# Eight heads' scores and v's weight summary as 64x32 pieces, in an attention with two expert layers

## The chip, the cores and the metric

The kernel runs on one core of a Trainium2 chip. The time is device microseconds of one execution. A profile comes from one more execution, with every engine's instructions recorded. The engines are TensorE (PE, with its weight loads as PEld), VectorE (DVE), ScalarE (ACT), GpSimd (POOL) and SyncE (SP), which issues the transfers.

## What is computed

```python
# q, k, v: (8, 8, 576, 64)   phi: (8, 8, 576, 32)
a = phi - np.max(phi, axis=2, keepdims=True)
a = np.exp(a)
a = a / (np.sum(a, axis=2, keepdims=True) + 1e-09)
k_m = np.einsum('bhsm,bhsd->bhmd', a, k)
v_m = np.einsum('bhsm,bhsd->bhmd', a, v)
scores = scale * np.matmul(q, k_m.transpose(0, 1, 3, 2))
scores = scores - np.max(scores, axis=-1, keepdims=True)
attn = np.exp(scores)
attn = attn / (np.sum(attn, axis=-1, keepdims=True) + 1e-09)
x = np.matmul(attn, v_m)      # heads side by side: (4608, 512)
h = x @ w_in                  # (4608, 2048)
x = (h * (1.0 / (1.0 + np.exp(-1.702 * h)))) @ w_out
h = x @ w2_in
out = (h * (1.0 / (1.0 + np.exp(-h)))) @ w2_out
```

There are 8 batches of 8 heads. A head's k and v are summed over the sequence into 32 rows of 64 each (the summaries), and q is scored against k's.

## The kernel before

**Two layers.** The first part of the program runs attention and the first expert layer together, in 256 slots; a batch has 32, a half sequence (288 tokens, `HS`) 16. In a slot, `first1` makes one block of 128 of the 2048 hidden features with six matmuls (L386: two groups of four heads, three products of high and low halves each), `gate` passes it through tanh (ScalarE, L360), one VectorE step (L361), a rounded copy (ScalarE, L364) and the rest (POOL, L366), and two slots later (`LAG`) `second1` multiplies it by the output weights with twelve matmuls (L398). The second expert layer follows from slot 256 on (from about 820 us), in another form, and has no part in the change.

**Attention's matmuls are folded into the first weight.** attn @ v_m @ w_in is computed as attn @ (v_m @ w_in). `wp_mm` (L276) makes that product w', 512 hidden features at a time (`c`, four of them) and four heads at a time (`g`, two); `wp_hi` (ScalarE, L281) and `wp_lo` (VectorE, L285) split it into a rounded half and the rest, the `slab`, which L386 reads as its stationary side. The moving side is `attnT`, the softmax of the scores, transposed.

**How heads lie.** `kv_mm` (L185) makes the summaries of four heads at once, each in 32 columns of the array, so a bank holds four heads x 32 rows. `kv_norm` divides by the sums and writes each row twice, side by side, once in the first and once in the second 64 columns; a mask (0 or 1 by partition) keeps one of the two, so that after the transposition by `kv_t` and the copy by `kv_e` a pair of heads stands block by block in `kvT`. One matmul over 128 rows (two heads x 64) and 64 columns then serves a pair of heads: `scores` (L230) and `wp_mm` (L276) each make two of them for four heads, one into each half of the partitions of one PSUM bank. `q_t` (L220) transposes q by pairs of heads, `q_e` copies that into `qT`.

**Softmax.** `soft1` transposes the scores out of PSUM in 32x32 blocks (VectorE, L242), takes the maximum (L244) and subtracts it (L245); `soft_exp` is on ScalarE; `soft2` sums, divides and transposes back; `soft_hi` and `soft3` split the result into `attnT`.

**PSUM.** All of attention's matmuls share two banks in turn (`ps_a`, 2 buffers, taken by `psa()`). A bank is free again when its reader on ScalarE or VectorE is through.

**What sets the order.** Tables of slot numbers. In a slot, the steps planned for "e" are written first, then `first1`, the steps for "p" (attention's matmuls), those for "l", `second1` of two slots ago, and those for "d" (transfers, all on SP's queue in the order written). `W0`, `W1`, `WS` hold w's slots of batch 0, of batch 1 and of the later ones, `QS` those of q, `SC` those of scores, `soft1` and `soft2`, counted from the batch's own start `z`; `ATT0`, `Q0` are for batch 0, which begins 46 slots ahead of slot 0. Up to slot 33 a scheduler may reorder the steps; from slot 34 on (`MANUAL`) each engine runs them as written.

Of the kernel before, what the change touches and what calls it, by code (L numbers as in the profile page):

```python
# [8 lines left out]
F32 = mybir.dt.float32  # L9
# [5 lines left out]
ALU = mybir.AluOpType  # L15
# [6 lines left out]
def attn_moe_moe(ctx: ExitStack, tc: tile.TileContext, q, k, v, phi, w1i, w1o, w2i, w2o, out):  # L22
    nc = tc.nc
    B, H, S, D = q.shape
# [167 lines left out]
    def kv_norm(b, g):  # L192
        a = st.pop(("kvps", b, g))
        rs = att.tile([128, 2], F32, tag="rs", name="rs", bufs=2)
        nc.vector.tensor_scalar(out=rs[:, 0:1], in0=a[:, 2 * D:2 * D + 1], scalar1=1e-9, scalar2=None, op0=ALU.add)
        nc.vector.reciprocal(out=rs[:, 1:2], in_=rs[:, 0:1])
        kvb = att.tile([128, 2, 2, D], F32, tag="kvb", name="kvb")
        keep = mask.rearrange("p (s o) -> p s o", o=1).to_broadcast([128, 2, D])
        for i in range(2):
            x = a[:, i * D:(i + 1) * D].rearrange("p (o d) -> p o d", o=1).to_broadcast([128, 2, D])  # L200
            nc.vector.scalar_tensor_tensor(out=kvb[:, i], in0=x, scalar=rs[:, 1:2], in1=keep,
                                           op0=ALU.mult, op1=ALU.mult)
        st["kvb", b, g] = kvb

    def kv_t(b, g):
# [14 lines left out]
            nc.tensor.transpose(a[:, c * P:(c + 1) * P], src[:, c], ident[:P, :P])  # L220

    def q_e(b, hf, p):
        t = att.tile([128, P, C3], F32, tag="qT", name="qT", bufs=3)
        nc.scalar.copy(out=t, in_=st.pop(("qp", b, hf, p))[:, 0:HS].rearrange("p (c s) -> p s c", c=C3))
        st["qT", b, hf, p] = t

    def scores(b, hf, g):
        a = st["sp", b, hf, g] = psa()
        for i in range(2):
            nc.tensor.matmul(out=a[64 * i:64 * i + 64, 0:HS],  # L230
                             lhsT=st["kvT", b, g][:, 0, 64 * i:64 * i + 64],
                             rhs=st.pop(("qT", b, hf, 2 * g + i)).rearrange("p s c -> p (s c)"),
                             start=True, stop=True)

    NG = HS // 32

# [33 lines left out]
        t = attnT[b, hf]  # L270
        (nc.gpsimd if b else nc.vector).tensor_tensor(out=t[:, g, 1], in0=x, in1=rd(t[:, g, 0]), op=ALU.subtract)

    def wp_mm(b, c, g):
        a = st["wp", b, c, g] = psa()
        for i in range(2):
            nc.tensor.matmul(out=a[64 * i:64 * i + 64], lhsT=st["kvT", b, g][:, 1, 64 * i:64 * i + 64],  # L276
                             rhs=w1[:, 2 * g + i, c * 512:(c + 1) * 512], start=True, stop=True)

    def wp_hi(b, c, g):
        t = slab[b, c, g] = moe.tile([128, 2, 512], F32R, tag="slab", name="slab", bufs=8)  # L280
# [409 lines left out]

    A0 = -46
    INIT = 'PABwwCDwwqqqq'
    Q0 = (-25, -14, -10, -7, -2, 0, 3, 3)
    LQ0 = (-7, -7, -4, 0)
    ATT0 = ((-9, -8, -7), (-6, -5, -3), (1, 2, 6), (5, 6, 7))


    LOAD = (None, None, None, None, -15, -15, -14, -10, -10, -9, -10, -8, -7, -5, -5, -4, -1, -3, 0, 1, 1, 4, 6,
# [29 lines left out]
    def plan_attention(b, z):  # L728
        for g in range(2):
            at(z - 2 + g, "e", phi_max, b, g)  # L730
        at(z + 1, "p", phi_max_t, b)
        at(z + 2, "e", phi_max_r, b)
        at(z + 3, "p", phi_max_b, b)
        for g in range(2):
            at(z + 4 + g, "e", phi_sub, b, g)
            at(z + 5 + g, "e", phi_exp, b, g)
            at(z + 6 + g, "e", phi_sum, b, g)
        for g, (k0, k1, n, t, e) in enumerate(KV):
            at(z + k0, "p", kv_mm, b, g, 0)
            at(z + k1, "p", kv_mm, b, g, 3)  # L740
            at(z + n, "e", kv_norm, b, g)
            todo.setdefault((z + t, "p"), []).insert(0, (kv_t, (b, g)))
            at(z + e, "e", kv_e, b, g)
        at(z + 10, "d", load_kv, b, 1, 0)
        at(z + 11, "d", load_kv, b, 1, 3)
        if b + 1 < B:
            at(z + 14, "d", load_kv, b + 1, 0, 0)
            at(z + 15, "d", load_kv, b + 1, 0, 3)
            at(z + 15, "d", load_phi, b + 1)
        for n in range(8):  # L750
            at(z + QS[n], "p", q_t, b, n // 4, n % 4)
            at(z + QS[n] + 1, "e", q_e, b, n // 4, n % 4)
            at(z + (QS[n - 2] if n > 1 else 2 + n), "d", load_q, b, n // 4, n % 4)
        for n, (p, s1, s2) in enumerate(SC):
            at(z + p, "p", scores, b, n // 2, n % 2)
            at(z + s1, "e", soft1, b, n // 2, n % 2)
            at(z + s1, "l", soft_exp, b, n // 2, n % 2)
            at(z + s2, "e", soft2, b, n // 2, n % 2)
            at(z + s2, "l", soft_hi, b, n // 2, n % 2)
            at(z + s2 + 1, "e", soft3, b, n // 2, n % 2)  # L760

    def plan_first(z):

        for g in range(2):
            at(z, "e", phi_max, 0, g)
            at(z + 3, "e", phi_sub, 0, g)
            at(z + 3, "l", phi_exp, 0, g)
            at(z + 4, "e", phi_sum, 0, g)
        at(z + 1, "p", phi_max_t, 0)
        at(z + 2, "e", phi_max_r, 0)  # L770
        at(z + 2, "p", phi_max_b, 0)
        for g in range(2):
            at(z + 4 + g, "p", kv_mm, 0, g, 0)
            at(z + 4 + g, "p", kv_mm, 0, g, 3)
            at(z + 5 + g, "e", kv_norm, 0, g)
            at(z + 6 + g, "p", kv_t, 0, g)
            at(z + 7 + g, "e", kv_e, 0, g)
        at(0, "d", load_phi, 1)
        at(5, "d", load_kv, 1, 0, 0)
        at(5, "d", load_kv, 1, 0, 3)  # L780
        for n in range(8):
            at(Q0[n], "p", q_t, 0, n // 4, n % 4)
            at(Q0[n] + 1, "e", q_e, 0, n // 4, n % 4)
            if n > 3:
                at(LQ0[n - 4], "d", load_q, 0, n // 4, n % 4)
        for n, (p, s1, s2) in enumerate(ATT0):
            at(p, "p", scores, 0, n // 2, n % 2)
            at(s1, "e", soft1, 0, n // 2, n % 2)
            at(s1, "l", soft_exp, 0, n // 2, n % 2)
            at(s2, "e", soft2, 0, n // 2, n % 2)  # L790
            at(s2, "l", soft_hi, 0, n // 2, n % 2)
            at(s2 + 1, "e", soft3, 0, n // 2, n % 2)

    def plan_wprime(b, n, s):
        a = (b,) + divmod(n, 2)
        at(s, "p", wp_mm, *a)
# [16 lines left out]
    for x in INIT:  # L813
# [42 lines left out]
    z = 32 * (B - 1) + 5  # L856
# [159 lines left out]
```

## Time and profile before

| what | |
|---|---|
| median of three runs | 1579.01 us (1578.94 to 1579.07) |
| the profiled execution | 1581.45 us |
| its span, first to last instruction | 1579.7 us |
| PE busy | 1511.9 us |
| DVE busy | 1010.7 us |
| ACT busy | 765.2 us |
| POOL busy | 567.9 us |
| w' matmuls (L276), 256 records | 72.8 us |
| scores matmuls (L230), 128 records | 25.9 us |

A float32 matmul leaves two records on PE, one for each of its passes. Busy time counts a stretch once, however many instructions overlap in it, and the ends of matmuls are modelled, so what a step costs TensorE is better read from the distance between starts than from its busy time.

### The profile page before, as it was taken

The page shows a single profiled execution, that of the slowest core. Times are in us where ns is not written, and L with a number is a line of the kernel's source. Part 1 is how long each engine was busy: PE and PEld are TensorE (multiplying, and loading weights), DVE is VectorE, ACT ScalarE, POOL GpSimd, SP SyncE. Part 2 cuts the span into 40 slices and gives each one's busy share as a digit, 9 for nine tenths or more (in the row PEclk, how much of TensorE's full clock was granted, in tenths as well). Part 3 has the DMA queues.
Part 4 walks back from the last instruction along what each step waited for, and adds up shares of the span by engine and source line. Part 5 has one row for each costly group of instructions (what it writes and reads, how often), then busy time and mean ns, then how long its engine had stood idle before and what let it go on. Part 6 is the DMA issues. An engine that isn't in the chain of part 4 may idle for free.

```text
span 1579.7 us, 29100 instructions
## 1 busy us (share of the span) xinstructions
PE 1511.9 (96%) x11104; PEld 1406.2 (89%) x11104; DVE 1010.7 (64%) x1552; ACT 765.2 (48%) x1539; POOL 567.9 (36%) x469
## 2 busy tenths in 40 slices
PE   4799999999999999999999999999996999999998
PEld 2578898888989889898998999999986999999998
DVE  6996546365473554635467656556577788878875
ACT  4664344454454445444455554555554344444443
POOL 2764334344343444433322323123124343142140
PEclk9899999999999999999999999999998999999999
DMA  9652242523525244221124334334455325335230
GB/s 283 182 163 65 57 130 71 158 76 94 139 87 145 69 125 112 89 62 42 60 75 155 121 134 147 110 141 147 135 191 175 118 93 191 104 107 191 89 122 31
DMA packets 174156, 189.08 MB, mean 120 GB/s; under 512 B 50112, under 2 KB 161728, under 8 KB 174016
## 3 DMA queue, kind: packets, MB, share of 16 engines
q1 hardware_dynamic: 174016, 187.22, 38.5%
q8 instruction: 87, 1.43, 0.4%
q14 instruction: 53, 0.43, 0.1%
HBM read 122.16 MB, written 65.01 MB: 118 GB/s over the span
## 4 chain that ended last, share of the span: by engine, by line
PE 79%; DVE 7%; issue 4%; ACT 4%; DMA 3%; POOL 2%; SPq 1%; DVEq 0%; ACTq 0%; POOLq 0%
PE y L398 23%; PE p L646 21%; PE h L386 11%; PE xb L533 9%; PE y L533 6%; PE a L276 3%; PE a L185 2%; PE a L230 1%; DVE e L435 1%; ACT xq L523 1%; PE a L220 1%; DMA raw<-in_moe_w_out_dram 1%; ACT gq L542 1%; DMA wst<-w2s 1%; POOL r L435 1%
## 5 line engine op out<-in xcount | busy, mean ns | idle before, releaser
L398 PE MATMUL y<-gh,wo 128*128 128x288 f32 x2048 | 460.1, 301 | 0.4 <-ACT gh L364 0.3
L398 PEld LDWEIGHTS y<-gh,wo 128*128 128x128 f32 x2048 | 341.4, 188 | 52.2 <-issue 25.8
L646 PE MATMUL p<-wq,op 128*128 128x256 f32 x3024 | 367.3, 284 | 14.0 <-ACT op L631 9.6
L646 PEld LDWEIGHTS p<-wq,op 128*128 128x128 f32 x3024 | 365.0, 191 | 16.4 <-ACT op L631 10.5
L366 POOL TENSOR_TENSOR gl<-g,gh 128x288 fp32r<-128x288 f32 x256 | 225.6, 882 | 425.3 <-ACT gh L364 386.1
L398 PE MATMUL y<-gl,wo 128*128 128x288 f32 x1024 | 301.9, 295 | 2.5 <-POOL gl L366 2.5
L361 DVE SCALAR_TENSOR_TENSOR g<-g,h 128x288 f32<-128x288 f32 x256 | 114.7, 449 | 289.5 <-ACT g L360 288.8
L438 DVE TENSOR_TENSOR op<-r,op 128x768 fp32r<-128x768 f32 x168 | 225.7, 1365 | 74.9 <-ACT op L631 74.3
L386 PE MATMUL h<-attnT,slab 128*128 128x288 f32 x1536 | 250.7, 298 | 12.9 <-ACT attnT L266 4.9
L386 PEld LDWEIGHTS h<-attnT,slab 128*128 128x128 f32 x1536 | 219.1, 189 | 19.0 <-ACT attnT L266 6.8
L533 PE MATMUL xb<-xq,wq 128*128 128x384 f32 x1152 | 220.7, 340 | 11.9 <-ACT e L583 7.2
L631 ACT CAST op<-r 128x768 fp32r<-128x768 f32 x168 | 139.3, 837 | 169.4 <-PE p L646 122.4
L533 PEld LDWEIGHTS xb<-xq,wq 128*128 128x128 f32 x1152 | 201.4, 189 | 19.9 <-ACT e L583 12.2
L360 ACT ACTIVATE g<-h 128x288 f32<-128x288 f32 x256 | 104.1, 407 | 191.3 <-PE h L386 185.4
L398 PEld LDWEIGHTS y<-gl,wo 128*128 128x128 f32 x1024 | 192.8, 188 | 4.4 <-POOL gl L366 3.4
L364 ACT CAST gh<-g 128x288 fp32r<-128x288 f32 x256 | 110.7, 433 | 167.9 <-DVE g L361 167.9
L533 PE MATMUL y<-xq,wq 128*128 128x384 f32 x864 | 166.1, 336 | 0.0
L533 PEld LDWEIGHTS y<-xq,wq 128*128 128x128 f32 x864 | 151.5, 188 | 0.3 <-ACT e L594 0.3
L542 ACT ACTIVATE gq<-e 128x384 f32<-128x384 f32 x144 | 75.0, 526 | 135.8 <-DVE e L435 134.5
L435 POOL TENSOR_TENSOR r<-r 128x768 f32<-128x768 f32 x24 | 55.9, 2353 | 193.7 <-DMA r<-gs 193.6
L547 DVE SCALAR_TENSOR_TENSOR gq<-gq,e 128x384 f32<-128x384 f32 x144 | 97.1, 680 | 35.1 <-ACT gq L542 29.7
L438 POOL TENSOR_TENSOR xq<-xr,xq 128x768 fp32r<-128x768 f32 x20 | 38.5, 1926 | 134.0 <-ACT xq L523 134.0
(111 smaller groups left out, 1535.2 us busy)
## 6 DMA issues: line engine op xcount, KB each, us to landing
gs<-gq SPq DMA_DIRECT2D x192, 192.0 KB, 1.9
r<-gs SPq DMA_DIRECT2D x192, 192.0 KB, 4.2
raw<-in_moe_w_out_dram SPq DMA_DIRECT2D x24, 512.0 KB, 4.3
raw<-in_moe_w_in_dram SPq DMA_DIRECT2D x18, 512.0 KB, 4.5
xr<-xs SPq DMA_DIRECT2D x24, 384.0 KB, 5.3
out_dram<-o SPq DMA_DIRECT2D x24, 384.0 KB, 3.6
q<-in_q_dram SPq DMA_DIRECT2D x124, 72.0 KB, 2.5
kv<-in_k_dram SPq DMA_DIRECT2D x30, 288.0 KB, 4.7
```

The source lines that it names most:

```text
L360: nc.scalar.activation(out=t[:, :n], in_=h[:, :n], func=ACTF.Tanh, scale=c)
L361: nc.vector.scalar_tensor_tensor(out=t[:, :n], in0=t[:, :n], scalar=1.0, in1=h[:, :n], op0=ALU.add, op1=ALU.mult)
L364: nc.scalar.copy(out=gh[:, :n], in_=t[:, :n])
L366: nc.gpsimd.tensor_tensor(out=gl[:, :n], in0=t[:, :n], in1=rd(gh[:, :n]), op=ALU.subtract)
L386: nc.tensor.matmul(out=h[:, :HS], lhsT=slab[b, f // 4, g][:, wi, f0:f0 + 128], rhs=x[:, g, xi], start=(g == 0 and n == 0), stop=(g == 1 an ...
L398: nc.tensor.matmul(out=ybank[d][:, :HS], lhsT=w[:, wi, d * 128:(d + 1) * 128], rhs=gg[gi][:, :HS], start=(f == fa and n == 0), stop=(f == ...
L438: eng.tensor_tensor(out=out, in0=a, in1=b, op=ALU.subtract)
L533: nc.tensor.matmul(out=out, lhsT=w[:, s, wi, f0:f0 + 128], rhs=x[:, s, xi], start=(start and s == 0 and k == 0), stop=(s == 1 and k == 2), ...
L542: nc.scalar.activation(out=t, in_=h, func=ACTF.Tanh)
L547: nc.vector.scalar_tensor_tensor(out=t, in0=t, scalar=1.0, in1=h, op0=ALU.add, op1=ALU.mult)
L631: nc.scalar.copy(out=t[:, :, 0], in_=s)
L646: nc.tensor.matmul(out=out[:, d], lhsT=t[:, u, gi, d * 128:(d + 1) * 128], rhs=w[:, u, wi], start=(start and d != 1 and p == 0 and u == 0 ...
```

## The change

A matmul of attention now takes one head: 64 rows and 32 columns of the array. A new function, `pairs`, writes eight of them, for all eight heads, over four column strips (`j`) and two row halves (`s`); those of the first row half go to one PSUM bank and those of the second to the other. `scores` and `wp_mm` call it, so each is one step for eight heads where it was two steps for four. A bank now holds the four even heads or the four odd ones, in scores and in w' alike. The two copies that `kv_norm` writes are both kept, in one VectorE instruction and without the mask, and `kvb` shares the buffer of `at`. `qT` gets a fourth buffer. The steps have new slots.

```diff
-        kvb = att.tile([128, 2, 2, D], F32, tag="kvb", name="kvb")
-        keep = mask.rearrange("p (s o) -> p s o", o=1).to_broadcast([128, 2, D])
-        for i in range(2):
-            x = a[:, i * D:(i + 1) * D].rearrange("p (o d) -> p o d", o=1).to_broadcast([128, 2, D])
-            nc.vector.scalar_tensor_tensor(out=kvb[:, i], in0=x, scalar=rs[:, 1:2], in1=keep,
-                                           op0=ALU.mult, op1=ALU.mult)
+        kvb = att.tile([128, HS], F32, tag="at", name="kvb")[:, 0:4 * D].rearrange("p (i s d) -> p i s d", i=2, s=2)
+
+        x = a[:, 0:2 * D].rearrange("p (i o d) -> p i o d", i=2, o=1).to_broadcast([128, 2, 2, D])
+        nc.vector.tensor_scalar(out=kvb, in0=x, scalar1=rs[:, 1:2], scalar2=None, op0=ALU.mult)
...
-    def scores(b, hf, g):
-        a = st["sp", b, hf, g] = psa()
-        for i in range(2):
-            nc.tensor.matmul(out=a[64 * i:64 * i + 64, 0:HS],
-                             lhsT=st["kvT", b, g][:, 0, 64 * i:64 * i + 64],
-                             rhs=st.pop(("qT", b, hf, 2 * g + i)).rearrange("p s c -> p (s c)"),
-                             start=True, stop=True)
+    def pairs(b, i, out, rhs, n):
+
+
+        for j in range(4):
+            for s in range(2):
+                h, r = (2 * j + s) % 4, slice(64 * s, 64 * s + 64)
+                nc.tensor.matmul(out=out[s][32 * j:32 * j + 32, 0:n],
+                                 lhsT=st["kvT", b, j // 2][r, i, 32 * h:32 * h + 32], rhs=rhs[j][r],
+                                 start=True, stop=True)
+
+    def scores(b, hf):
+        a = [psa() for _ in range(2)]
+        for g in range(2):
+            st["sp", b, hf, g] = a[g]
+        pairs(b, 0, a, [st.pop(("qT", b, hf, j)).rearrange("p s c -> p (s c)") for j in range(4)], HS)
...
-    def wp_mm(b, c, g):
-        a = st["wp", b, c, g] = psa()
-        for i in range(2):
-            nc.tensor.matmul(out=a[64 * i:64 * i + 64], lhsT=st["kvT", b, g][:, 1, 64 * i:64 * i + 64],
-                             rhs=w1[:, 2 * g + i, c * 512:(c + 1) * 512], start=True, stop=True)
+    def wp_mm(b, c):
+        a = [psa() for _ in range(2)]
+        for g in range(2):
+            st["wp", b, c, g] = a[g]
+        pairs(b, 1, a, [w1[:, j, c * 512:(c + 1) * 512] for j in range(4)], 512)
...
-    WS = (20, 23, 27, 29, 31, 34, 38, 39)
+    WS = (21, 26, 32, 38)
...
-    QS = (12, 16, 18, 20, 24, 27, 28, 30)
-    SC = ((18, 19, 23), (23, 24, 26), (29, 30, 34), (31, 32, 35))
+    QS = (10, 14, 16, 17, 23, 24, 25, 27)
+    SC = ((19, 22, 24), (29, 35, 37))
...
+    def plan_softmax(b, hf, z, p, *s2):
+        at(z + p, "p", scores, b, hf)
+        for g in range(2):
+            at(z + p + 1, "l" if b and g else "e", soft1, b, hf, g)
+            at(z + p + 1 + (b and g), "e" if b and g else "l", soft_exp, b, hf, g)
+            at(z + s2[g], "e", soft2, b, hf, g)
+            at(z + s2[g], "l", soft_hi, b, hf, g)
+            at(z + s2[g] + 1, "e", soft3, b, hf, g)
...
-        at(s + 1, "e", wp_hi, *a)
-        if b:
-            at(s + 2, "e", wp_lo, *a)
-        else:
-            at(s + 1, "l", wp_lo, *a)
+    def plan_wprime(b, c, s):
+        at(s, "p", wp_mm, b, c)
+        for g in range(2):
+            at(s + 1, "e", wp_hi, b, c, g)
+            at(s + 1, "e" if b else "l", wp_lo, b, c, g)
```

TensorE in slot 87 of the kernel before (batch 3): a block of the first matrix product, a pair of scores, a pair of w', and on to the second product (`y` are its sums, `gh` the gate's rounded half).

```order
L398 MATMUL y_3747<-gh,wo_533 128x288
L386 MATMUL h<-attnT,slab 128x288 x6
L230 MATMUL a<-qT,kvT 64x288 x2
L276 MATMUL a<-w_83,kvT 64x512 x2
L398 MATMUL y_3735<-gh,wo_535 128x288
```

TensorE in slot 83 of the changed kernel, the same batch's first scores, and behind it in slot 85 its first w'; the line numbers are the changed kernel's (L391 and L403 are L386 and L398).

```order
L403 MATMUL y_3813<-gh,wo_292 128x288
L391 MATMUL h<-attnT,slab 128x288 x6
L230 MATMUL a<-qT,kvT 32x288 x8
L403 MATMUL y_3801<-gh,wo_357 128x288
L403 MATMUL y_3801<-gl,wo_357 128x288
```

```order
L403 MATMUL y_3813<-gh,wo_359 128x288
L391 MATMUL h<-attnT,slab 128x288 x6
L230 MATMUL a<-w_82,kvT 32x512 x8
L403 MATMUL y_3801<-gh,wo_364 128x288
L403 MATMUL y_3801<-gl,wo_364 128x288
```

Two matmuls of 64 columns have become eight of 32, and scores and w' no longer stand in one slot. From slot 21 to slot 231 TensorE's order has 64 places with L230 or L276 before (28 pairs of scores, 56 of w'), and 42 after (14 and 28 steps of eight matmuls); in a batch from the third on, nine and six.

VectorE in slots 82 to 86 of the kernel before: the end of a weight conversion, one softmax start (L242 to L245), the gates of slots 83 to 85 (L361), the rest of a w' (L285).

```order
L86 SCALAR_TENSOR_TENSOR stg<-raw,stg 128x512
L242 STREAM_TRANSPOSE nat<-a 128x288
L244 TENSOR_REDUCE mx<-nat 128x9
L245 TENSOR_TENSOR nat<-nat,mx 128x288
L361 SCALAR_TENSOR_TENSOR g<-g,h 128x288 x3
L285 TENSOR_TENSOR slab<-a,slab 128x512
```

VectorE in slots 83 to 85 of the changed kernel (L366 is the gate step; L247, L249, L250 are the softmax start).

```order
L366 SCALAR_TENSOR_TENSOR g<-g,h 128x288
L247 STREAM_TRANSPOSE nat<-a 128x288
L249 TENSOR_REDUCE mx<-nat 128x9
L250 TENSOR_TENSOR nat<-nat,mx 128x288
L366 SCALAR_TENSOR_TENSOR g<-g,h 128x288
L247 STREAM_TRANSPOSE nat<-a 128x288
L249 TENSOR_REDUCE mx<-nat 128x9
L250 TENSOR_TENSOR nat<-nat,mx 128x288
L366 SCALAR_TENSOR_TENSOR g<-g,h 128x288
```

The second group's softmax start now follows the first's with one gate between them.

## Rows read from the trace of the kernel before

**Rows 1.** The page, part 1: busy us, share of the span and instructions of each engine.

```profile
PE 1511.9 (96%) x11104; PEld 1406.2 (89%) x11104; DVE 1010.7 (64%) x1552; ACT 765.2 (48%) x1539; POOL 567.9 (36%) x469
```

**Rows 2.** Busy by stretch: PE, PEld, DVE, ACT, POOL (counts); clock; DMA share; GB/s.

```profile
65.00:100.00 35.00, 32.44 (x229) 26.73 (x227) 34.93 (x54) 23.93 (x51) 25.28 (x22) 1.00 0.52 148
...
130.00:175.00 45.00, 45.00 (x320) 38.92 (x319) 23.66 (x49) 19.38 (x48) 14.18 (x18) 1.00 0.18 50
...
367.00:462.00 95.00, 95.00 (x756) 84.69 (x755) 51.53 (x105) 45.74 (x109) 39.92 (x43) 1.00 0.39 110
```

**Rows 3.** Chain of waits, 0 to 140: start us, us, what was waited for.

```profile
0.74 5.24 DMA phi<-in_phi_dram
...
127.94 1.09 PE h L386 x6
```

**Rows 4.** PE in order of time, 405 to 521: start us, us, operation.

```profile
406.01 0.95 PE L386 MATMUL h<-attnT,slab 128*128 128x288 f32 x6
...
408.38 0.95 PE L386 MATMUL h<-attnT,slab 128*128 128x288 f32 x6
...
411.84 0.96 PE L386 MATMUL h<-attnT,slab 128*128 128x288 f32 x6
...
422.87 0.95 PE L386 MATMUL h<-attnT,slab 128*128 128x288 f32 x6
...
426.92 0.96 PE L386 MATMUL h<-attnT,slab 128*128 128x288 f32 x6
...
429.58 0.69 PE L386 MATMUL h<-attnT,slab 128*128 128x288 f32 x4
...
518.53 0.95 PE L386 MATMUL h<-attnT,slab 128*128 128x288 f32 x6
```

**Rows 5.** PE in order of time, 455 to 462.

```profile
456.59 0.96 PE L386 MATMUL h<-attnT,slab 128*128 128x288 f32 x6
...
460.17 0.95 PE L386 MATMUL h<-attnT,slab 128*128 128x288 f32 x6
```

**Rows 6.** All engines in order of time, 475 to 480.

```profile
474.91 0.95 PE L386 MATMUL h<-attnT,slab 128*128 128x288 f32 x6
...
475.79 0.59 PEld L185 LDWEIGHTS a<-kv,phi 96*32 96x32 f32 x24 [0.16 <-issue]
...
478.27 0.96 PE L386 MATMUL h<-attnT,slab 128*128 128x288 f32 x6
```

**Rows 7.** PEld in order of time, 456 to 459.

```profile
457.48 0.20 PEld L276 LDWEIGHTS a<-w,kvT 128*64 128x64 f32 x4 [0.17 <-DVE sm L256]
```

**Rows 8.** Groups by line and shape: count, busy us, mean ns, idle before.

```profile
L366 POOL TENSOR_TENSOR gl<-g,gh 128x288 fp32r<-128x288 f32 x256 | 225.6, 882 | 425.3 <-ACT gh L364 386.1 <-PE a L276 12.9 <-issue 11.0
...
L361 DVE SCALAR_TENSOR_TENSOR g<-g,h 128x288 f32<-128x288 f32 x256 | 114.7, 449 | 289.5 <-ACT g L360 288.8
...
L360 ACT ACTIVATE g<-h 128x288 f32<-128x288 f32 x256 | 104.1, 407 | 191.3 <-PE h L386 185.4 <-POOL gl L366 3.5 <-POOL stg L88 1.7
...
L285 DVE TENSOR_TENSOR slab<-a,slab 128x512 fp32r<-128x512 f32 x64 | 43.6, 682 | 1.6 <-ACT slab L281 1.6
...
L281 ACT CAST slab<-a 128x512 fp32r<-128x512 f32 x64 | 37.3, 583 | 2.2 <-PE a L276 1.5
...
L245 DVE TENSOR_TENSOR nat<-nat,mx 128x288 f32<-128x288 f32 x32 | 26.8, 837 | 1.0
...
L242 DVE STREAM_TRANSPOSE nat<-a 128x288 f32<-128x288 f32 x32 | 15.2, 475 | 2.3 <-PE a L230 2.3
...
L244 DVE TENSOR_REDUCE mx<-nat 128x9 f32<-128x288 f32 x32 | 14.5, 454 | 1.0
...
L201 DVE SCALAR_TENSOR_TENSOR kvb<-a,rs,mask 128x128 f32<-128x128 f32 x32 | 9.8, 346 | 0.5
```

**Rows 9.** SP's issues, 427 to 431, and the page's row on q's transfers.

```profile
428.17 1.22 SPq L129 DMA_DIRECT2D q<-in_q_dram  x2
...
q<-in_q_dram SPq DMA_DIRECT2D x124, 72.0 KB, 2.5
```

More of the change, by code (lines that the diff above doesn't have):

```diff
@@ L48, in attn_moe_moe @@
     ident = const.tile([128, 128], F32)
-    mask = const.tile([128, 2], F32)
     ones = const.tile([128, 1], F32)
@@ L222, in q_e @@
     def q_e(b, hf, p):
-        t = att.tile([128, P, C3], F32, tag="qT", name="qT", bufs=3)
+        t = att.tile([128, P, C3], F32, tag="qT", name="qT", bufs=4)
         nc.scalar.copy(out=t, in_=st.pop(("qp", b, hf, p))[:, 0:HS].rearrange("p (c s) -> p s c", c=C3))
         st["qT", b, hf, p] = t
-    def scores(b, hf, g):
-        a = st["sp", b, hf, g] = psa()
-        for i in range(2):
-            nc.tensor.matmul(out=a[64 * i:64 * i + 64, 0:HS],
-                             lhsT=st["kvT", b, g][:, 0, 64 * i:64 * i + 64],
-                             rhs=st.pop(("qT", b, hf, 2 * g + i)).rearrange("p s c -> p (s c)"),
-                             start=True, stop=True)
+    def pairs(b, i, out, rhs, n):
[10 more added lines that the diff above has]
+        pairs(b, 0, a, [st.pop(("qT", b, hf, j)).rearrange("p s c -> p (s c)") for j in range(4)], HS)
     NG = HS // 32
@@ L692, in attn_moe_moe @@
     INIT = 'PABwwCDwwqqqq'
-    Q0 = (-25, -14, -10, -7, -2, 0, 3, 3)
+    Q0 = (-25, -14, -10, -7, -1, 0, 3, 3)
     LQ0 = (-7, -7, -4, 0)
-    ATT0 = ((-9, -8, -7), (-6, -5, -3), (1, 2, 6), (5, 6, 7))
+    ATT0 = ((-6, -4, -3), (4, 6, 7))
     LOAD = (None, None, None, None, -15, -15, -14, -10, -10, -9, -10, -8, -7, -5, -5, -4, -1, -3, 0, 1, 1, 4, 6,
@@ L706, in attn_moe_moe @@
     POOLF = (1, 3, 5, 7, 12, 14)
-    W0 = (-4, -2, 1, 2, 10, 13, 14, 15)
-    W1 = (18, 25, 28, 29, 32, 33, 39, 41)
-    WS = (20, 23, 27, 29, 31, 34, 38, 39)
+    W0 = (-3, 2, 13, 15)
+    W1 = (26, 31, 37, 39)
+    WS = (21, 26, 32, 38)
     Z1 = 5
     KV = ((8, 9, 10, 11, 12), (12, 13, 14, 15, 16))
-    QS = (12, 16, 18, 20, 24, 27, 28, 30)
-    SC = ((18, 19, 23), (23, 24, 26), (29, 30, 34), (31, 32, 35))
+    QS = (10, 14, 16, 17, 23, 24, 25, 27)
+    SC = ((19, 22, 24), (29, 35, 37))
+    SC1 = (SC[0], (29, 32, 34))
     W2 = 45
@@ L753, in plan_attention @@
             at(z + (QS[n - 2] if n > 1 else 2 + n), "d", load_q, b, n // 4, n % 4)
[L754 to L760, printed above, removed]
+        for hf in range(2):
+            plan_softmax(b, hf, z, *(SC1 if b == 1 else SC)[hf])
+    def plan_softmax(b, hf, z, p, *s2):
[6 more added lines that the diff above has]
+            at(z + s2[g] + 1, "e", soft3, b, hf, g)
     def plan_first(z):
@@ L785, in plan_first @@
                 at(LQ0[n - 4], "d", load_q, 0, n // 4, n % 4)
[L786 to L796, printed above, removed]
-        at(s + 1, "e", wp_hi, *a)
-        if b:
-            at(s + 2, "e", wp_lo, *a)
-        else:
-            at(s + 1, "l", wp_lo, *a)
+        for hf in range(2):
+            plan_softmax(0, hf, 0, *ATT0[hf])
+    def plan_wprime(b, c, s):
[3 more added lines that the diff above has]
+            at(s + 1, "e" if b else "l", wp_lo, b, c, g)
     make_identity(nc, ident)
     nc.vector.memset(ones, 1.0)
-    for j in range(4):
-        for s in range(2):
-            nc.vector.memset(mask[32 * j:32 * j + 32, s:s + 1], 1.0 if j % 2 == s else 0.0)
     w1s = [[(kk, j) for kk in range(4)] for j in range(4)]
@@ L833, in attn_moe_moe @@
             plan_attention(b, 32 * (b - 1) + (Z1 if b == 1 else 0))
-        for n in range(8):
+        for n in range(4):
             plan_wprime(b, n, (W0, W1)[b][n] if b < 2 else 32 * (b - 1) + WS[n])
```

## Prediction, made before the changed kernel ran

> **What bounds the kernel now.** I read the page first: PE is busy 96% of the span, DVE 64%, ACT 48%, POOL 36% [rows 1]. An average hides stages, so the second view is the busy time by stretch [rows 2]. From 65 to 100 us VectorE is busy 34.93 of 35 us: the start is VectorE's, which turns the raw weights into float32. In 130:175 it is TensorE that has no gap, 45.00 of 45, and the same in 367:462, 95.00 of 95. From 820 us on the second expert layer runs, which the change does not touch. The chain of waits begins with 5.24 us for phi's transfer, and it passes over to TensorE alone at 127.94 us, in slot 21 (a slot is one block of six L386 matmuls and the twelve of L398 behind it) [rows 3]. So what TensorE saves counts from slot 21 to slot 231, where attention's last step lies; before that it counts where VectorE happens not to be late.
>
> The third view is TensorE in order of time. The distance between two blocks of L386 is a slot's length. With nothing else in it a slot takes 408.38 - 406.01 = 2.37 us. What a visit of attention adds is the rest [rows 4, 5]:
> - q's three transposes: 429.58 - 426.92 - 2.37 = 0.29.
> - q and a pair of scores: 411.84 - 408.38 - 2.37 = 1.09, so the scores alone 0.80.
> - one w' pair (L276, v's summary times w1): 460.17 - 456.59 - 2.37 = 1.21.
> - scores and w' in one visit: 426.92 - 422.87 - 2.37 = 1.68.
>
> From the last three: the scores' own stream is 1.68 - 1.21 = 0.47, w's is 1.68 - 0.80 = 0.88, and the rest, 0.80 + 1.21 - 1.68 = 0.33, is paid once a visit, whatever is in it: it is the change of shape from 128x128 and back. A batch of 32 slots confirms it: 518.53 - 422.87 = 95.66 us, 75.84 of it slots, 19.8 attention; nine visits x 0.33, 4 x 0.47 and 8 x 0.88 are 11.9 of that, and q, k/v's summary and phi's maximum the rest.
>
> **What 64x32 pieces can do, from rows.** The visit of 24 records for k and v's summaries (L185: 96 rows x 32 columns, four column strips, each with its own moving data of 128 columns) takes 478.27 - 474.91 - 2.37 = 0.99 us [rows 6]. In w's stream a pass of 512 columns takes 0.44 (each pair is two passes, 4 records), so 128 columns take 0.11, and 24 in turn would be 2.6. The visit less 0.33 is 0.66, six passes of 0.11: four strips run at once, at the full rate, with no dearer visit. That the two row halves also run at once, no row shows. For it: each half writes a bank of its own, reads partitions of its own, and a float32 pass moves 288 columns in 0.47 / 2 = 0.235 us where L398's takes 2.37 / 18 = 0.13, so two float32 streams together write little faster than one stream of L398 does now. I take it that all eight run at once; both ends stand with the rivals.
>
> The Trainium skill, in TensorEngine Tiling (Array Packing), sections Available Configurations and Key Properties, lists 64x32 as eight tiles that load and multiply independently; no run here shows that, and by it the sum would be the one below.
>
> **The sum.** Before, from slot 21: TensorE's order has 28 pairs of scores, 56 of w' and 64 visits: 28 x 0.47 + 56 x 0.88 + 64 x 0.33 = 13.2 + 49.3 + 21.1 = 83.6 us. After: 14 scores and 28 w', all eight heads in the time of one pair, in 42 visits, six a batch in place of nine (none holds two steps any more): 6.6 + 24.6 + 13.9 = 45.1. Eight pieces start one after another; per visit I take 0.03 (24 loads take 0.59 us and 4 take 0.20, 0.02 for each more, and most of them lie under a pass) [rows 6, 7]; bounds 0 and 0.1. That is 1.3. **Saved: 83.6 - 46.4 = 37 us.** q's transposes stay eight a batch at 0.29.
>
> **What else changes, at or near nothing.**
> - kvb: two masked multiplies of 0.346 [rows 8] become one plain one over 256. Bounds: 0.346 (half the width) and 0.69 (the two); I take 0.52, half way, since both are the same reading of PSUM and only the width differs. VectorE gains 0.17 x 16 = 2.7; from slot 21 on it waits for TensorE, so 0. The eight memsets of the mask lie under phi's 5.24 us: 0.
> - The start: VectorE has the same conversions, the same four softmax pieces and eight slab pieces, one of these (0.682) behind slot 21 in place of ahead of it. The first softmax half now waits for all four q transposes; both then run behind one another. Bounds: the 2 x 0.47 + 4 x 0.88 = 4.5 us of batch 0's streams that fall away, if all of it lay on the path, and as much lost if the first slots' order turns out badly. I take 0, nearest to the rows in which VectorE is full.
> - Both banks of `ps_a` are taken by one step, so scores wait until the last user of either is read, with second1's twelve matmuls queued behind them on TensorE. Tightest is slot 83 to 85 (scores, then w' two slots on). From slot 83's start the scores end at 6 x 0.13 + 0.80 = 1.6; VectorE needs 0.475 + 0.454 + 0.837 = 1.77 for the first half, to 3.4. Slot 84 starts at 3.2; its gate step (L361, 0.45) can start 0.95 (h) + 0.41 (tanh) later, with 0.1 for the hand-overs at 4.66, and ends at 5.1; then the second half's transpose, 5.6. w' wants the bank at 3.2 + 2.37 + 0.79 = 6.4: 0.8 spare. Behind w' in slot 90, q in slot 91 wants a bank 3.6 + 0.8 = 4.4 after slot 90's start; the gate (0.95 + 0.41 + 0.45, and ScalarE's copy, no longer than 0.58), then the slab's copy (0.583) and VectorE's subtraction (0.682) give it back at 3.7: 0.7 spare [rows 4, 8]. Cost 0; if the cover is short it is rival C.
> - The gate: from a slot's first matmul h 0.95, tanh 0.41, L361 0.45, copy 0.58 at most, POOL 0.88, 3.3 us, against 2 x 2.37 + 0.79 = 5.5 until second1 reads it. What VectorE puts ahead of one L361 is at most a softmax step and two slab pieces (slot 86), 1.77 + 1.36 = 3.1 us if an end is as long as a start; it begins when the L361 of the slot before is through, and would have to run 2.2 us late.
> - q's loads move with QS on SP's queue. Tightest is the seventh: issued behind the transposes of slot 87, wanted in slot 89. Behind a visit of 0.29 the two DMAs take 1.22 to issue and land 2.5 after it [rows 9]: 4.0 us, against 2 x 2.66 = 5.3. Cost 0.
>
> The profiled execution took 1581.45 us, 1.75 of it around the span; less 37 it would be 1544. The three runs' median, 1579.01, lies 2.4 below it, so **1542**.
>
> **Rivals.**
> A. The row halves take turns. Then streams are as before and only visits fall away: 22 x 0.33 - 1.3 = 6: 1573. For it: no row has two halves at once. Against: the rates above.
> B. Slower: a strip's weights can't be loaded while its half multiplies. Then a step is four passes, not one: 4 x 31.2 + 13.9 + 1.3 = 140 against 83.6, +56: 1635. It decides where eight pieces take more than (83.6 - 15.2) / 31.2 = 2.2 passes; with all eight in turn it would be far worse. Against it: four loads are through in 0.20 us, before the first pass of 0.44 can end, and 24 loads in 0.59 of a visit of 0.99 [rows 6, 7], all in the same rows of the array.
> C. The pieces run at once, but VectorE gives the second bank back late. Where the second half's transpose stands one more block of 1.77 back, TensorE waits 1.77 - 0.8 = 1.0 at each of 14 scores: 14 us, 1556. For it: both halves' softmax now follow at once. Against: VectorE has 0.8 spare there, and is busy 51.53 of 95 us.
>
> Rival B is what the Trainium skill says in TensorE: Matmul & The Clock Gate (Part 3, The mechanism): loads overlap running matmuls only where the row groups differ. By that rule it would be 1635; the loads of rows 6 and 7 speak against it.
>
> **How the numbers follow.** Forecast 0.80, C 0.08, A 0.07, B 0.05. The range: down, 4 for the start, 1.3 for the starts of the pieces and 2 for reading visits to 0.05, to 1534; up to C, 1556. It leaves out A and B, 0.12, and some of C. Faster by over 0.2% (which is about what a measurement of this kernel tells from none): forecast, C and most of A, 0.93; within it, A with a bad start, 0.02; slower, B, 0.05.
>
> **What would show it.** The eight records of a pass start within some 0.06 us; a w' visit still makes its slot about 3.6 us long, a scores visit 3.2; the period of 32 slots falls from 95.7 to about 90.3; slot 21 still starts near 128 us; the first layer ends some 37 us earlier and the rest is as long as now. It would be wrong if L230's second half starts a pass later than its first (A), if its loads spread over the passes (B), if TensorE waits for L242 or the slab at slots 85, 91 or 96 (C), or if slot 21 moves by more than 4 us.

## The result, and the profile after

| | us |
|---|---|
| before, median of five runs beside it | 1579.01 (1578.87 to 1579.51) |
| after, median of five runs | 1587.15 (1584.49 to 1589.85) |
| ratio | 1.0051, 95% interval 1.0036 to 1.0066 |
| profiled execution of after, and its span | 1587.46, 1585.7 |

The change makes the kernel 0.5% slower. Forecast were 1542 us and a range of 1534 to 1556, so the forecast was wrong by 45 us and in its sign.

The matmuls do what was forecast. Part 1 of the page of after (busy us, share, instructions) answers to [rows 1]:

```profile
PE 1490.0 (94%) x11488; PEld 1398.4 (88%) x11488; DVE 1009.9 (64%) x1528; ACT 763.1 (48%) x1539; POOL 564.4 (36%) x469
```

TensorE is busy 22 us less than before, in a span that is 6 us longer. TensorE in order of time around a visit of scores and one of w' (start us, us, operation; L386 is now L391, L398 is L403, and both steps run through `pairs`, L230), and the weight loads of the second visit:

```profile
416.14 0.95 PE L391 MATMUL h<-attnT,slab 128*128 128x288 f32 x6
417.02 0.72 PE L230 MATMUL a<-qT,kvT 64*32 64x288 f32 x16
...
419.36 0.96 PE L391 MATMUL h<-attnT,slab 128*128 128x288 f32 x6
...
421.73 0.98 PE L391 MATMUL h<-attnT,slab 128*128 128x288 f32 x6
422.64 1.09 PE L230 MATMUL a<-w,kvT 64*32 64x512 f32 x16
...
425.35 0.95 PE L391 MATMUL h<-attnT,slab 128*128 128x288 f32 x6
```

```profile
422.64 0.18 PEld L230 LDWEIGHTS a<-w,kvT 64*32 64x32 f32 x16 [0.18 <-issue]
```

With eight heads in it a scores slot takes 419.36 - 416.14 = 3.22 us and a w' slot 425.35 - 421.73 = 3.62, as they did with half as many [rows 4, 5]. All eight pieces run at once.

What the stages did instead stands in the busy time by stretch of after (us, then PE, PEld, DVE, ACT, POOL with counts, granted clock, DMA share, GB/s), which answers to [rows 2]:

```profile
130.00:175.00 45.00, 43.92 (x369) 40.28 (x370) 23.89 (x53) 21.45 (x55) 15.93 (x20) 1.00 0.18 48
367.00:462.00 95.00, 92.19 (x813) 84.28 (x812) 52.68 (x105) 45.65 (x111) 41.18 (x44) 1.00 0.38 107
...
522.86:531.81 8.95, 7.06 (x34) 4.21 (x35) 7.83 (x16) 3.64 (x9) 4.01 (x4) 0.63 0.27 88
613.16:622.74 9.58, 3.98 (x21) 3.77 (x20) 2.59 (x6) 3.57 (x9) 3.18 (x3) 0.72 0.35 102
```

TensorE, which had no gap before, has gaps now. The last two lines are one slot each, 149 and 178, of 8.95 and 9.58 us where a slot takes 2.4 to 3.6.

Cut at the start of slot 21 and of slot 255, the spans compare like this (the column of e1 is the first experiment below):

| stretch | before | forecast | after | e1 |
|---|---|---|---|---|
| to slot 21 | 127.94 | 127.9 | 133.07 | 134.39 |
| slot 21 to slot 255 | 689.46 | 652.5 | 694.04 | 662.26 |
| from slot 255 | 762.3 | 762.3 | 758.6 | 758.1 |
| span | 1579.7 | 1542.7 | 1585.7 | 1554.7 |

The cuts are these rows, first of before, then of after, then of e1 (TensorE in order of time):

```profile
817.40 0.55 PE L386 MATMUL h<-attnT,slab 128*128 128x288 f32 x3
```

```profile
133.07 1.06 PE L391 MATMUL h<-attnT,slab 128*128 128x288 f32 x6 [0.98 <-DVE g L366]
...
827.11 0.55 PE L391 MATMUL h<-attnT,slab 128*128 128x288 f32 x3
```

```profile
134.39 0.40 PE L391 MATMUL h<-attnT,slab 128*128 128x288 f32 x1 [0.98 <-DVE g L366]
...
796.65 0.42 PE L391 MATMUL h<-attnT,slab 128*128 128x288 f32 x2
```

So after misses the forecast by 5.1 us at the start and by 41.6 us between slots 21 and 255, and gains 3.7 behind.

**Where TensorE waits.** The waits by engine and releaser from 130 to 820 us (us in total, times, longest), after:

```profile
PE y L403 <- DVE o L382: 5.6, 1, 5.6
PE h L391 <- DVE g L366: 4.8, 3, 2.0
PE a L230 <- DVE phi L163: 4.0, 3, 2.8
PE a L230 <- DVE nat L247: 3.6, 3, 1.7
PE a L217 <- DVE slab L290: 2.3, 2, 1.5
PE a L144 <- DVE slab L290: 2.1, 3, 1.0
```

With six smaller ones they are 28.5 us; the same view of before has three, 1.4 us in all. The releasers are of many kinds, VectorE's steps in softmax, gate and slab, so I asked what VectorE had waited for. Slots 145 to 149 in order of time, cut to what matters:

```profile
512.36 3.05 SPq L419 DMA_DIRECT2D xs<-o  x4
515.50 1.23 SPq L128 DMA_DIRECT2D q<-in_q_dram  x2
...
516.78 0.59 SPq L60 DMA_DIRECT2D raw<-in_moe_w_out_dram  x1
...
520.82 0.66 ACT L76 ACTIVATE stg<-raw 128x512 f32<-128x512 f32 x1 [5.74 <-DMA raw<-in_moe_w_out_dram]
...
521.92 0.39 ACT L365 ACTIVATE g<-h 128x288 f32<-128x288 f32 x1
522.35 0.45 DVE L366 SCALAR_TENSOR_TENSOR g<-g,h 128x288 f32<-128x288 f32 x1 [7.73 <-ACT g L365]
...
522.86 1.05 PE L391 MATMUL h<-attnT,slab 128*128 128x288 f32 x6 [2.02 <-DVE g L366]
...
524.31 1.09 PE L230 MATMUL a<-w,kvT 64*32 64x512 f32 x2 [0.41 <-DVE nat L247]
...
526.88 1.95 PE L230 MATMUL a<-w,kvT 64*32 64x512 f32 x14 [1.48 <-DVE nat L247]
```

Read it from the top. SP issues its transfers in the order written: four stores of the first layer's output (`xs`, which wait for `o`), a load of q, and behind them a load of the second layer's raw weights (`w2_load`, 32 of them, one each five slots, planned in "d" of slot 45 + 5n for a conversion in "e" of two slots later). It was planned for slot 145, which ends at 512.66 us; it is issued 4.1 us behind that and lands 4.0 us after its issue. ScalarE has reached that conversion (L76) 5.74 us before it can start, and behind it stand the gate's tanh (L365) of two slots. VectorE's gate step waits 7.73 us for it, and TensorE for VectorE: first L391, then w', which wants a bank that VectorE could not yet read. The Trainium skill, Perfetto Trace Analysis, section Tensor Engine Instruction, calls ScalarE and VectorE strict first-in-first-out; these rows agree: the tanh, whose input L391 had left long before, starts only behind L76.

ScalarE's waits for raw in the same stretch, after and then before:

```profile
ACT stg L76 <- DMA raw<-in_moe_w_in_dram: 19.8, 8, 5.1
ACT stg L76 <- DMA raw<-in_moe_w_out_dram: 16.2, 5, 5.7
```

```profile
ACT stg L77 <- DMA raw<-in_moe_w_out_dram: 8.5, 6, 3.3
ACT stg L77 <- DMA raw<-in_moe_w_in_dram: 7.6, 4, 2.7
```

They were 16 us before, none over 3.3, and TensorE lost next to nothing by them; now they are 36 us, up to 5.7. In 12 of the 13 waits of after, loads of q stand in the unbroken run of issues on SP ahead of raw (slot 65 is the exception, with stores alone); in before they do so in 7 of 10. For half of the 36 us SP was held at the load of q itself, until q's transposes had read the buffer; for the other half it was held at the stores first, as here.

### The profile page after: what moved, and what is told of

The parts are those of the page before. It is cut to its first block, busy times and chain, and to the rows that moved or that the text cites. A ratio compares the mean times of both kernels' runs of the same rounds, so it can differ in the third digit from the quotient of the medians.

```text
span 1585.7 us, 29873 instructions
## 1 busy us (share of the span) xinstructions
PE 1490.0 (94%) x11488; PEld 1398.4 (88%) x11488; DVE 1009.9 (64%) x1528; ACT 763.1 (48%) x1539; POOL 564.4 (36%) x469
## 4 chain that ended last, share of the span: by engine, by line
PE 68%; DVE 13%; DMA 6%; ACT 6%; issue 4%; POOL 1%; SPq 1%; ACTq 0%; DVEq 0%; POOLq 0%
PE p L651 21%; PE y L403 18%; PE xb L538 9%; PE h L391 8%; PE y L538 6%; DMA raw<-in_moe_w_in_dram 2%; PE a L230 2%; PE a L184 1%; DVE g L366 1%; DMA raw<-in_moe_w_out_dram 1%; DVE e L440 1%; ACT xq L528 1%; DVE pm L137 1%; DVE stg L85 1%; DMA kv<-in_v_dram 1%
## 5 line engine op out<-in xcount | busy, mean ns | idle before, releaser
L403 PE MATMUL y<-gh,wo 128*128 128x288 f32 x2048 | 466.4, 304 | 6.7 <-DVE o L382 5.6
L403 PEld LDWEIGHTS y<-gh,wo 128*128 128x128 f32 x2048 | 345.6, 190 | 46.1 <-issue 19.3
L403 PE MATMUL y<-gl,wo 128*128 128x288 f32 x1024 | 304.1, 297 | 4.0 <-POOL gl L371 4.0
L366 DVE SCALAR_TENSOR_TENSOR g<-g,h 128x288 f32<-128x288 f32 x256 | 114.8, 449 | 282.0 <-ACT g L365 281.8
L391 PE MATMUL h<-attnT,slab 128*128 128x288 f32 x1536 | 251.9, 299 | 19.5 <-ACT attnT L271 13.7
L391 PEld LDWEIGHTS h<-attnT,slab 128*128 128x128 f32 x1536 | 221.0, 191 | 28.4 <-ACT attnT L271 18.0
L403 PEld LDWEIGHTS y<-gl,wo 128*128 128x128 f32 x1024 | 195.2, 191 | 5.3 <-POOL gl L371 4.9
L365 ACT ACTIVATE g<-h 128x288 f32<-128x288 f32 x256 | 104.3, 408 | 147.1 <-PE h L391 142.7
```

The source lines that it names most:

```text
L365: nc.scalar.activation(out=t[:, :n], in_=h[:, :n], func=ACTF.Tanh, scale=c)
L366: nc.vector.scalar_tensor_tensor(out=t[:, :n], in0=t[:, :n], scalar=1.0, in1=h[:, :n], op0=ALU.add, op1=ALU.mult)
L391: nc.tensor.matmul(out=h[:, :HS], lhsT=slab[b, f // 4, g][:, wi, f0:f0 + 128], rhs=x[:, g, xi], start=(g == 0 and n == 0), stop=(g == 1 an ...
L403: nc.tensor.matmul(out=ybank[d][:, :HS], lhsT=w[:, wi, d * 128:(d + 1) * 128], rhs=gg[gi][:, :HS], start=(f == fa and n == 0), stop=(f == ...
```

## Experiments

Two theories. **Theory 1, the queue:** q's new slots put the loads of raw weights later in SP's order; ScalarE waits for them in its own order, and TensorE with it. **Theory 2, the banks:** each step of attention now takes both banks of `ps_a`, so TensorE waits for whoever reads them last, late raw weights or not. Each run of the kernel before beside these experiments gave a median of 1577.7 to 1578.9 us.

**e1: raw two slots earlier.**

```diff
-            at(s, "d", w2_load, m, n)
+            at(s - 2, "d", w2_load, m, n)
```

> Changed kernel (1587.2 us) with one edit: the transfers of the second layer's raw weights stand two slots earlier on SP's queue. Theory 1 (queue order: the moved q loads now stand ahead of these transfers on SP, ScalarE reaches its conversion before they land and holds everything behind it): ScalarE's wait for them after 130 us falls from 36 us to under 6, the long slots 69, 149 and 178 lose their excess, and the time falls by 18 to 25 us, to 1562 to 1569. Theory 2 (two banks at once: TensorE waits for whichever reader of the two is later, conversions or not): ScalarE's wait falls too, but TensorE's waits for the bank stay, and the time falls by 6 us at most, to 1581 or more.

Measured: 1557.61 us, ratio 0.9867 (0.9852 to 0.9881). ScalarE's waits for raw are gone altogether, and one number in the plan has turned 0.5% slower into 1.3% faster. What is left of TensorE's waits from 130 to 820 us:

```profile
PE a L144 <- DVE slab L290: 2.1, 3, 1.0
PE a L206 <- DVE kvb L199: 1.4, 1, 1.4
PE a L184 <- DVE slab L290: 1.4, 1, 1.4
PE a L217 <- DVE slab L290: 1.2, 1, 1.2
PE a L230 <- DVE phi L163: 1.1, 2, 0.9
```

With three smaller ones they are 9.5 us. Theory 1 holds, and its price was above what I had expected of it.

**e2, e3, e4: the banks, raw left as it is.** e2 puts the copies out of w's banks first among the steps of their slot; e3 moves the last w' of a batch off the slot in which phi's maximum holds a bank; e4 moves batch 0's last two visits ahead of batch 1's summaries.

```diff
 # e2, in plan_wprime
+        if b:
+            todo.setdefault((s + 1, "e"), [])[0:0] = [(fn, (b, c, g)) for g in range(2) for fn in (wp_hi, wp_lo)]
+            return
...
-            at(s + 1, "e" if b else "l", wp_lo, b, c, g)
+            at(s + 1, "l", wp_lo, b, c, g)
 # e3
-    WS = (21, 26, 32, 38)
+    WS = (21, 26, 32, 39)
 # e4
-    W0 = (-3, 2, 13, 15)
+    W0 = (-3, 2, 9, 12)
```

> Changed kernel with one edit: from batch 1 on, the reading of w' out of its two banks stands first among a slot's early steps, ahead of softmax ends. Theory 2 (two banks): the waits for the slab pieces at slots 40, 65, 119, 123, 161 and 193, some 6 us together, go, and the time falls by 5 to 8 us, to 1579 to 1582. Theory 1 (queue order): they come from ScalarE's late conversions, so at most 2 us go: 1585 or more.

> Changed kernel with one edit: the last w' step of batches 2 to 7 stands one slot later (39 for 38 after the batch's start), when the bank with phi's maxima has been read. Theory 2 (two banks): the waits for phi's subtraction at slots 70 and 134 go, and with them some 3 to 5 us: 1582 to 1584. Theory 1 (queue order): the wait at slot 134 is a late conversion's, which then shows elsewhere: 1585 to 1587.

> Changed kernel with one edit: the third and fourth w' steps of batch 0 stand at slots 9 and 12 in place of 13 and 15, ahead of batch 1's summaries, which take a bank from slot 13 on. Theory 2 (two banks): the wait of 3.6 us for the summaries' reader in slot 15 goes, slot 21 starts near 128 us in place of 133, and the time falls by 3 to 5 us. Theory 1 (queue order): the start is bound by conversions as before, slot 21 stays at 132 to 134 us, and the time within 1.5 us of 1587.

Measured: 1589.72, 1589.32 and 1588.63 us; none differs from after by more than the runs of one kernel do. TensorE's waits in e3:

```profile
PE a L184 <- DVE slab L290: 7.2, 6, 1.8
...
PE a L230 <- DVE phi L163: 0.9, 1, 0.9
```

The waits for phi fall from 4.0 us in after to 0.9, and 5.8 us more stand at the next step that takes a bank: there a wait removed in one place turned up in another. In e4 slot 21 starts at 129.1 us and slot 255 at 823.4, both about 4 us earlier than in after, as theory 2 wants; but the profiled execution is the fastest of e4's four (1584.28 us), and the median shows no gain.

**b2: the kernel before, raw two slots earlier** (the edit of e1, in before).

> The kernel before, with the loads of the second layer's raw weights asked for two slots earlier, nothing else. It separates two readings of why that edit took 30 us off the changed kernel. Reading S (late raw weights cost time only because the changed kernel's slots are shorter and each batch's visits hold both banks of ps_a, so that TensorE is the first to miss what ScalarE does late): in the kernel before TensorE's waits above its regular ones from slot 21 on are only 1.7 us, so ScalarE's 16 us of waits for raw go to about 0 and the time stays within 2 us of 1579 (1577 to 1580). Reading G (a late raw load costs the same wherever it stands): 29.6 us for 36 us of waits in the changed kernel, so 16 us would give 13: 1566.

Measured: 1577.94 us, ratio 1.0000 (0.9990 to 1.0009). ScalarE's 16 us of waits for raw went to 0 there too, and nothing was gained. A late load costs only what the work around it cannot take up.

**b1: the kernel before with q's new slots alone; b3: the same with raw two slots earlier.**

```diff
-    QS = (12, 16, 18, 20, 24, 27, 28, 30)
+    QS = (10, 14, 16, 17, 23, 24, 25, 27)
-        t = att.tile([128, P, C3], F32, tag="qT", name="qT", bufs=3)
+        t = att.tile([128, P, C3], F32, tag="qT", name="qT", bufs=4)
```

(kvb moves into a buffer of tag `at`, as in after, to make room.)

> The kernel before with only the changed kernel's slots for q (QS = 10, 14, 16, 17, 23, 24, 25, 27, with the fourth qT buffer that they need and kvb in a buffer of tag at, as the changed kernel has them). Scores and v's summary times the input weight stay as they were. If moving q's loads on SP's queue is what makes the raw weights late (reading Q), ScalarE's waits for raw rise from 16 us towards 36, and the time rises by some us (1582 to 1590; how much depends on what slack the longer slots leave). If it is the shorter slots that make the same loads late (reading S), the waits stay at 16 +- 5 us and the time within 2 us of 1579.

> The kernel before with the changed kernel's slots for q (as b1, which took 1599.0) and raw asked for two slots earlier as well. If the price of q's new slots (21 us in b1) comes through late raw weights alone, it falls back to 1577 to 1580. If it comes from banks of ps_a (q's transposes now stand at other slots against the kernel before's scores and its v's summary times the input weight: 7.3 us of waits of TensorE in b1's trace at the latter), about 7 to 10 us stay: 1585 to 1588.

Measured: b1 1598.96 us, 1.4% slower (ratio 1.0141, 1.0124 to 1.0158); b3 1588.42 (1.0061, 1.0046 to 1.0076). ScalarE's waits for raw in b1 were

```profile
ACT stg L77 <- DMA raw<-in_moe_w_in_dram: 14.4, 7, 3.1
ACT stg L77 <- DMA raw<-in_moe_w_out_dram: 13.9, 5, 5.2
```

28.3 us against 16 in before, with not one matmul of the heads changed; the time is above the 1582 to 1590 us that were expected. So q's slots, with the buffers that came with them, make raw late. The loads that ScalarE waits for in b1 are those of twelve of after's thirteen slots. They raise the waits by 12 of the 20 us by which after raises them. The other 8 are mostly longer waits for the same loads (slot 65: 2.3 us in b1, 5.1 in after); that the shorter slots make them longer is likely, but no run tested it, and none gave the changed kernel q's old slots. b1 is 21.3 us over the kernel before beside it and b3 9.6, so some 12 come through raw. The other 10 stay in b3, whose listed waits of TensorE are 6.9 us, nearly all at banks, probably because the w' visits of before were laid out around other slots of q:

```profile
PE a L276 <- DVE nat L242: 5.2, 5, 2.3
```

**e7: a dose, raw one slot earlier in after** (`s - 1` for `s`).

> A dose: the changed kernel with the raw weights asked for one slot earlier (e1: two). If time follows ScalarE's waits for raw (36 us at 0 slots for 1587.2, 0 us at 2 slots for 1557.6, so 0.82 us of time for one of wait), a slot of some 2.8 us that takes most of each wait of 1 to 5.7 us leaves some 8 to 12 us of waits, and the time is 1564 to 1568. If it isn't these waits but another thing that two slots change (which transfers run side by side), there is no such middle: near 1587 or near 1557.

Measured: 1567.25 us, and 9.5 us of waits for raw are left. Three doses lie near a line: 36 us of waits give 1587.2, 9.5 give 1567.3, 0 give 1557.6; the straight line between the ends has 1565.4 at 9.5.

**e6, e5: what the banks are worth once raw is in time.** e6 is e1 and e4 together, e5 is e1 to e4 together.

> The changed kernel with raw asked for two slots earlier (as in e1) and batch 0's last two visits of v's summary times the input weight at slots 9 and 12 instead of 13 and 15 (as in e4). Theory 1 and 2 together: e4 moved slot 21 from 133.1 to 129.1 us, but late raw weights further on swallowed it; with those gone it should show in full: 1557.6 - 4 to 5 = 1552 to 1554, slot 21 at 129 to 130. If the two slots' position doesn't matter for the end (no gain kept, as e4 by itself read): 1557 +- 1.5.

> The changed kernel with four edits: raw two slots earlier, batch 0's visits at slots 9 and 12, v's summary's copies first among a slot's ScalarE and VectorE work, and batch 1's last visit a slot later (39 for 38) so that it doesn't meet the bank of phi's maxima. If, once raw comes in time, the bank waits left in e1's trace are real losses (slab 2.1 us, phi 1.06 us, first wait 3.6 us), it is 2 to 3 us under e6: 1549 to 1551. If such waits are absorbed elsewhere, it is e6 +- 1.5 us. It also tells which version is best.

Measured on one chip: e6 1554.03 us (0.9860, 0.9843 to 0.9876), e5 1560.43 (0.9896, 0.9881 to 0.9911). Together, the edits of e2 and e3 cost 6 us rather than gain 2 to 3: with the copies out of w's bank first and w' a slot later, the summaries of k and v (L184) wait for the slab at slots 104, 136 and 168, where they did not in e1.

**e8, e9: the kernels of e6 and e1 again, side by side.**

> The same kernel as e6 (raw two slots earlier, batch 0's last two visits at slots 9 and 12), beside e1's kernel on one chip, since 1554.0 against 1557.6 from two chips can't be told apart. If the wait for the k/v summary's bank at slot 15 is a real loss of the start (theory 2), this is 3 to 5 us under e1's kernel; if the start gives it back elsewhere (in e6's trace TensorE waits 2.1 us at slot 13 for the last columns of the input weight, 1.3 us at slot 18 for kv's transfer and 1.5 us each twice at slot 20 for the gate), within 1.5 us of it.

> The same kernel as e1 (raw two slots earlier alone), for the comparison with e8 on one chip: 1556 to 1559, slot 21 at 134 us.

Measured: e8 1555.13 us (1551.86 to 1557.41), e9 1556.01 (1555.09 to 1558.02). In the two profiles slot 21 starts at 128.9 and at 134.0 us, and the spans differ by nearly as much, 1550.1 and 1554.5. But the other runs of e8 spread up to e9's, and e6's profiled execution, 1559.0 us long, has slot 21 at 135.5; so a gain of moving the two visits is seen in single executions and is not settled as a median. Both are 1.4% faster than before; they are the best versions found.

## Why the prediction was wrong

**64x32 pieces: right.** The eight records of a pass start within 0.047 us (0.06 was forecast), the second pass 0.45 us later. Rivals A and B are false. The rule behind B, in the Trainium skill, TensorE: Matmul & The Clock Gate, Part 3 (The mechanism), would keep the second pass's loads of the same rows back, unless they go into the background weight buffer that the same section also names; all sixteen loads are through in 0.18 us, under the first pass, so here the measurement decides against the rule as rival B took it. The eight tiles that the Trainium skill lists in TensorEngine Tiling (Array Packing), Available Configurations and Key Properties, agree with the eight records within 0.047 us.

**The sum: right where nothing waits.** The 32 slots of e1 with the fewest waits, 192 to 223, run from

```profile
629.08 0.81 PE L391 MATMUL h<-attnT,slab 128*128 128x288 f32 x5
...
720.24 0.55 PE L391 MATMUL h<-attnT,slab 128*128 128x288 f32 x3
```

to the next: 91.2 us, and 0.56 of that is a wait for a bank at slot 193. Forecast were 90.3, down from 95.7. The four periods ahead of it take 91.9 to 92.4 us; most of what they have over this one is at the banks, below.

**q's loads: the step that failed.** I asked of QS on SP's queue only whether q itself comes in time, and costed it at nothing. It does come in time. What stands behind it on SP, a raw load, and who waits for that, was not asked. The rows needed were there: in before raw stands behind q's loads too, and ScalarE waits 16 us for it. This is the row behind the one on q in [rows 9], in the same view:

```profile
429.43 0.60 SPq L61 DMA_DIRECT2D raw<-in_moe_w_in_dram  x1
```

The cost was 31.8 us between slots 21 and 255 (after less e1). The profile places some 30 of it: TensorE's listed waits fell by 20 from after to e1 (28.5 against 9.5, of which 1.0 is already the second layer's), 3 are w' visits in slots 53, 58 and 70 that stop for their second bank without a line in that list (the next but one paragraph says why), and at most 6.6 are the clock, below. The rest I can't place.

**The gate: right in kind, short in size.** VectorE's gate step "would have to run 2.2 us late" before TensorE sees it. It ran over 5 us late, and not by a softmax block ahead of it on VectorE, which is what I had priced, but by ScalarE.

**Both banks of `ps_a`: costed at 0, about 8 us.** The two places that I worked out (slots 84 to 85 and 90 to 91) do hold in e1. Between slots 21 and 255 e1 is still 9.8 us behind the forecast. Its 9.5 us of waits, less 2.4 that end ahead of slot 21's first matmul (kvb and the gate) and 1.0 of the second layer, are 6.1, against 1.4 in before: 4.7 us more, at places that I had not looked at: w' behind phi's maximum (slot 37), and the summaries (40), phi's transposes (65, 161, 193) and q (119), each behind a slab copy. There is more that this list does not show. It counts time without a record of a matmul, and a visit whose second bank is late sends the first piece and then stops, so that this piece's records cover the first microsecond of the wait. In order of time in e1, slots 90 and 166, and ScalarE's copy of q that held the bank in slot 90:

```profile
335.81 2.18 PE L230 MATMUL a<-w,kvT 64*32 64x512 f32 x16
...
554.91 1.74 PE L230 MATMUL a<-w,kvT 64*32 64x512 f32 x16
```

```profile
336.46 0.39 ACT L221 COPY qT<-a 128x288 f32<-128x288 f32 x1
```

Undisturbed, such a visit takes 1.09 us. Those of slots 37, 90, 134 and 166 take 3.03, 2.18, 2.31 and 1.74: 4.9 us more, of which the list has 1.1. That leaves 3.8 us, and both together are 8.5 of the 9.8. This is rival C's mechanism, a bank given back late, at other slots, held by q's copy and phi's steps as well as by the slab, and at some 60% of its price. What remains, 1 to 2 us, is some 0.2 a period, no more than the rounding of the sum's terms.

**The start: the bound was 4.5, it was 5.1.** Slot 15 does it. In after the second bank of a w' visit is held there by batch 1's summary until kvb is made, and the matmuls behind that wait run at the half clock level; the row of the same slot in before, where TensorE waits 1.68 us, stands first:

```profile
107.40 1.08 PE L276 MATMUL a<-w,kvT 128*64 128x512 f32 x4 [1.68 <-DVE slab L285]
```

```profile
110.52 1.93 PE L230 MATMUL a<-w,kvT 64*32 64x512 f32 x8 [3.61 <-DVE kvb L199]
...
113.02 0.44 PE L403 MATMUL y<-gl,wo 128*128 128x288 f32 x1
113.26 0.68 PE L403 MATMUL y<-gh,wo 128*128 128x288 f32 x2
113.74 0.44 PE L403 MATMUL y<-gl,wo 128*128 128x288 f32 x1
```

At slots 5 and 10 both kernels stood within 1.4 us of each other, at slot 16 after was 4.8 behind. e4 and e8, which move that visit, bring slot 21 back to 129.1 and 128.9.

**The second layer** was to take as long as before; it is 3.7 us shorter in after and 4.2 in e1. Up to 1.7 of it is a stretch of 3.4 us at the half clock level in before, at 860 us, that neither after nor e1 has; no run looked at the rest.

## What to carry over

When a table of slots moves a transfer, ask who stands behind it on its queue, and what the consumer of that transfer holds up in its own order; a load two slots earlier was worth 30 us here. A wait that costs nothing in a kernel with slack (16 us of it in before, worth 0.0% by b2) can fall due when the plan around it changes. Take the earliest releaser in such a chain first: as long as it stood, three edits of later waits showed no gain in the median. With it gone two of the three, together, cost 6 us, so a wait at a bank is no proof that time is lost there.

## What the runs showed of the hardware

TensorE's granted clock fell with the three longest waits after slot 21 (2.8, 2.0 and 5.6 us, in slots 134, 149 and 178), which made them dearer than they were. In the window 522.86:531.81 above it is 0.63 of full speed on average, a mixture of 2.4 and 1.2 GHz. At the half level three records of L403 take 113.74 - 113.02 = 0.72 us, 0.24 each, where the prediction read 0.13 at the full level. Between slots 21 and 255 of after the clock was down in three stretches, here by busy time as above:

```profile
477.39:480.81 3.42, 3.42 (x15) 3.42 (x16) 2.03 (x4) 2.37 (x5) 2.09 (x3) 0.50 0.10 42
525.18:532.01 6.83, 5.35 (x28) 3.47 (x28) 5.82 (x12) 2.92 (x7) 2.17 (x3) 0.50 0.35 115
617.34:624.17 6.83, 4.45 (x18) 4.34 (x18) 2.59 (x6) 2.39 (x8) 3.18 (x3) 0.50 0.38 118
```

In the rest of after, as in all of before and e1 between the same slots, it is 1.00. At half speed TensorE's 13.2 busy us did the work of 6.6, so the lower level cost at most 6.6 us; where TensorE waits it costs nothing. The same holds at the start: from 110 to 130 us, behind the wait in slot 15, the granted clock of e9 is 0.83, and that of e8, whose TensorE does not wait in that slot, 1.00.
